# A two-layer memory-attention network on one core: the order in which the steps are recorded, from a list scheduler to a list in the source

## The chip, the cores and the metric

The kernel runs on one core of a Trainium2 chip. The metric is the device time of one execution in microseconds, and the median of the runs where there are several. The profile is of one execution, taken by the hardware profiler; its span runs from the first to the last instruction.

## The reference

The input x has 2048 tokens of 640 features, in bf16. Two rounds of the same pair of blocks are computed, with the same weights:

```
x = x + A(layernorm(x));  x = x + B(layernorm(x));  x = x + A(layernorm(x));  x = x + B(layernorm(x))

A:  q, k, v = x @ wq, x @ wk, x @ wv          32 heads of 20 features, 4 segments of 512 tokens
    for each segment s, in order:
        a_dot = softmax(q k^T * scale + causal mask) @ v           inside the segment
        a_mem = (phi(q) @ M) / (phi(q) @ z + 1e-6)                 what earlier segments left
        o     = g * a_mem + (1 - g) * a_dot                        g = sigmoid(beta), for each head
        M    += phi(k)^T @ v;   z += sum(phi(k))                   phi(t) = t + 1 if t > 0, else exp(t)
    return o @ wo
B:  relu(x @ w1) @ w2                         w1: 640 x 1728, w2: 1728 x 640
```

## The kernel before

The work goes by round (a = 0, 1) and segment (s = 0 to 3), with 512 tokens in each of these eight parts. The heads are taken in groups of four, eight groups to a segment, and two groups share one pad.

The data takes this way in a part. Layernorm statistics are made on DVE (L795, L797), the reciprocal root on GpSimd (POOL, L811), the normalized tokens on DVE (L841) and their transposition by a DMA on SP's queue (`turn`, L817); for the first 512 tokens TensorE (PE) transposes (L866, `first_tile`). The projections of K and Q (`proj_first`, `proj_one`; copied out of PSUM at L981 by DVE or L982 by ACT) and of V (`proj_v`, L1036) are groups of matmuls (`group`, L774 and L777). `spill` (L1070) writes K and Q to a scratch in HBM and `fill` (L1117) reads them back into a pad, in four pieces for each pad, so that each head starts at its own quarter of the partitions; the first pad is filled directly (L1097). `scores` (L1301) multiplies K by Q on four row groups of PE at once, two halves at a time: 160 such pairs of halves in all, five to a pad. `exps` (L1365) takes the exponentials on ACT, `causal` (L1377) masks on POOL, `apply` (L1397, or by token at L1436 for two groups) multiplies by V on column groups, and the result is copied out (L1407), transposed by a DMA and divided (`divide`, L1483 to L1491). The memory is read by `mem_read` (L1180 to L1195), added by `combine` (L1510), and written by `mem_write` (L1238 to L1265) from phi(K) (`phi_`, L1144 to L1147). `turn_o` transposes the result in two DMAs, `out_proj` multiplies it by wo and DVE adds it to x (L1519). `ln_b` normalizes again, `ffn` does block B in groups of matmuls, with the relu on ACT (L1595) or DVE (L1594) and the sum into x on DVE (L1614); `ffn_rest` (L1572, L1579) does the last 64 columns of w1. `store` (L1646) writes out.

PE runs matmuls in three forms. A group of matmuls can be recorded full, 128 x 128, or quartered by columns, each matmul as four of 128 x 32 (`either` gives both; L774 is the full form, L777 the quartered one). `apply` is always quartered, `scores` always in row groups.

Each of these functions is a generator, a stream, that yields its steps one by one. A step names its engine, what it waits for and the buffer it takes. 39 streams are added in a fixed sequence, and a stream can spawn a child with steps of its own (the copy out of PSUM behind a group, for example). `Sched.run` records steps, one at a time, into the program of their engine. The engines then run freely against each other and are held only by semaphores. So the recording decides three things: the order of the steps on each engine (the DMA queue of SP among them), for a copy out of PSUM whether ACT or DVE does it, and for a group's matmul whether it is full or quartered.

The scheduler keeps estimated times for every step. At each turn it computes for the next step of every stream when it could start, adds a lateness where its data would only just be there (`_late`, `SOFT`, `SOFT_DMA`, the latter two from a certain score on), adds an offset from the table `SHIFT` for this stream, part and place, and records the step with the lowest sum:

```
key = (round(start + late + SHIFT.get(self.place(n, st[1]), 0)), 0.5 if op.urgent else prio, self.rank[id(st[1])], n)
if best is None or key < best[0]:
    best = (key, st, end, start, k, op)
```

Of the kernel before, what the change touches and what calls it, by code (L numbers as in the profile page):

```python
# [109 lines left out]
class Op:  # L110

    def __init__(self, alts, waits, dma=None, acq=None, urgent=False, take=(), mode="full", lag=0.0, port=False):
        self.lag = lag
# [8 lines left out]
        self.urgent = urgent  # L125
        self.take = take
        self.data = 0.0
# [32 lines left out]
class Spawn:  # L160
    def __init__(self, prio, gen):
        self.prio = prio
        self.gen = gen


LONE_NS = 300.0
SWITCH_NS = 96.0
COLS_LAG = 1500.0
SOFT = 400
SOFT_DMA = 1000  # L170
SOFT_FROM = ("sc",6,4,1)
SEM_NS = 60.0
PE_MARGIN = 80.0
HOLDERS = 1
SHIFT = {
# [45 lines left out]
class Sched:  # L221


    def __init__(self, prog):
# [9 lines left out]
        self.landed = set()  # L234
        self.met = {}
        self.seen = {}
        self.phase = {}
        self.made = {}
        self.held = {"dve": [], "pool": []}

# [1504 lines left out]
```

## Time and profile before

| | |
|---|---|
| median of 3 runs | 550.78 us (549.76 to 551.34) |
| the profiled execution | span 549.3 us; its time isn't given apart, the span lies 1.5 us under the median |
| PE busy | 539.8 us (98%), 9025 matmuls |
| DVE, ACT, POOL busy | 427.8, 406.0, 195.7 us |
| moved by DMA | 62.20 MB in 133325 packets |

The lines of the profile read like this: line of the kernel, engine, operation, what it writes and what it reads, shape, count, then busy time, mean duration in ns, and the engine's idle time ahead of it with what ended it. PE is matmul, PEld its weight load, SPq the issue of a DMA on SP's queue. A line of the instructions in order of time starts with its start and its length in us. In the waits the numbers are: us in total, times, longest us.

### The profile page before, as it was taken

What the parts mean: (1) busy time and instruction counts of PE and PEld (TensorE: products, weight loads), DVE (VectorE), ACT (ScalarE), POOL (GpSimd) and SP (SyncE); (2) the same over time, 40 slices, a digit from 0 to 9 for tenths busy, and PEclk for the clock granted to TensorE, in tenths of its full rate; (3) what the DMA queues carried; (4) which work ended last, traced back from release to release, by engine and by line L of the source; (5) the groups of instructions that cost most, each with busy time, mean ns of one, the idle gap of its engine ahead of it and who ended that gap; (6) DMA issues with size and microseconds to landing.
All of it is one profiled execution on the core that took longest, in us unless ns stands there. A gap on an engine that the chain in (4) does not pass through costs nothing.

```text
span 549.3 us, 20483 instructions
## 1 busy us (share of the span) xinstructions
PE 539.8 (98%) x9025; PEld 305.5 (56%) x9025; DVE 427.8 (78%) x1067; ACT 406.0 (74%) x516; POOL 195.7 (36%) x305
## 2 busy tenths in 40 slices
PE   7999999999999999999999999999999999999997
PEld 6543464455554546646556555564646654757656
DVE  4899999898999989898778858997899788417102
ACT  5699899789888987788888867897778787350130
POOL 5255444333453334443433423433333333201000
PEclk9999999999999999999999999999999999999999
DMA  8699979715384175438384743336246511541201
GB/s 270 165 198 253 245 158 223 221 44 116 89 165 98 40 180 77 75 68 120 47 212 93 116 116 93 58 69 104 50 139 130 117 32 22 106 63 33 71 2 51
DMA packets 133325, 62.20 MB, mean 113 GB/s; under 512 B 112116, under 2 KB 123124, under 8 KB 133236
## 3 DMA queue, kind: packets, MB, share of 16 engines
q1 hardware_dynamic: 132672, 60.36, 51.5%
q8 instruction: 71, 1.16, 0.9%
q10 hardware_dynamic: 564, 0.53, 0.4%
q14 instruction: 18, 0.15, 0.1%
HBM read 20.56 MB, written 12.85 MB: 61 GB/s over the span
## 4 chain that ended last, share of the span: by engine, by line
PE 88%; ACT 6%; DVE 2%; DMA 2%; SPq 1%; issue 0%
PE ps L774 35%; PE ps L777 35%; PE ps L1301 8%; PE ps L1397 6%; ACT PT L1365 5%; PE ps L1180 2%; DMA x_sb<-in_A_x_dram 1%; PE ps L1572 1%; PE ps L1238 1%; DMA pad<-scr 1%; SPq L602 1%; DVE xn_tok L841 0%; SPq L612 0%; DVE stats L795 0%; DVE x_sb L1614 0%; DVE o_sb L1491 0%
## 5 line engine op out<-in xcount | busy, mean ns | idle before, releaser
L1365 ACT ACTIVATE PT<-ps 128x1024 bf16<-128x1024 f32 x320 | 308.9, 1028 | 59.3 <-PE ps L1301 57.6
L1377 POOL TENSOR_SCALAR_AFFINE_SELECT PT<-PT 128x512 bf16<-128x512 bf16 x256 | 169.3, 679 | 241.1 <-ACT PT L1365 241.0
L777 PE MATMUL ps<-xnT,w_r 128*32 128x512 bf16 x1256 | 76.0, 379 | 0.0
L777 PE MATMUL ps<-w_r,hT 128*32 128x320 bf16 (+1 forms) x1764 | 67.8, 295 | 0.0
L1614 DVE TENSOR_TENSOR x_sb<-x_sb,ps 128x320 bf16<-128x320 bf16 (+1 forms) x65 | 30.7, 474 | 43.6 <-PE ps L777 38.7
L1301 PE MATMUL ps<-pad 20*128 20x512 bf16 (+3 forms) x1024 | 63.4, 301 | 1.2 <-ACT PT L1365 0.7
L774 PE MATMUL ps<-w_r,hT 128*128 128x320 bf16 x404 | 64.2, 300 | 0.0
L795 DVE BATCH_NORM_STATS2 stats<-x_sb 128x6 f32<-128x320 bf16 x124 | 55.0, 478 | 3.8 <-DMA x_sb<-in_A_x_dram 3.0
L777 PEld LDWEIGHTS ps<-w_r,hT 128*32 128x32 bf16 x1764 | 45.2, 97 | 12.6 <-issue 1.4
L1595 ACT ACTIVATE hT<-ps 128x512 bf16<-128x512 f32 x50 | 29.9, 599 | 29.0 <-PE ps L777 25.6
L774 PE MATMUL ps<-xnT,w_r 128*128 128x512 bf16 x206 | 50.8, 380 | 0.0
L774 PEld LDWEIGHTS ps<-w_r,hT 128*128 128x128 bf16 x404 | 37.6, 98 | 19.4 <-issue 4.9
L1301 PEld LDWEIGHTS ps<-pad 20*128 20x128 bf16 x1024 | 17.9, 92 | 52.9 <-issue 24.5
L777 PEld LDWEIGHTS ps<-xnT,w_r 128*32 128x32 bf16 x1256 | 31.6, 97 | 27.8 <-issue 2.0
L1519 DVE TENSOR_TENSOR x_sb<-x_sb,ps 128x320 bf16<-128x320 bf16 x64 | 29.7, 478 | 20.4 <-PE ps L777 16.0
L811 POOL TENSOR_TENSOR rstd<-lnU,mhalf 128x2 f32<-128x2 f32 (+2 forms) x27 | 21.1, 782 | 63.5 <-DVE lnU L807 60.4
L1407 DVE CAST otu<-ps 128x512 bf16<-128x512 f32 x52 | 35.6, 685 | 9.1 <-PE ps L1397 8.2
L1397 PE MATMUL ps<-PT,v_aug 128*21 128x128 bf16 (+3 forms) x896 | 40.3, 300 | 0.0
L1594 DVE TENSOR_SCALAR hT<-ps 128x512 bf16<-128x512 f32 x54 | 36.5, 681 | 1.7 <-PE ps L774 0.7
L1491 DVE TENSOR_TENSOR o_sb<-otk,rden 128x320 bf16<-128x320 bf16 x62 | 34.8, 588 | 0.5
L981 DVE CAST stg<-ps 128x512 bf16<-128x512 f32 (+1 forms) x37 | 24.7, 669 | 12.5 <-PE ps L774 6.3
L1146 ACT ACTIVATE stg<-stg 128x512 bf16<-128x512 bf16 x50 | 31.7, 635 | 2.0 <-DVE rtmp L1144 1.8
(118 smaller groups left out, 731.5 us busy)
## 6 DMA issues: line engine op xcount, KB each, us to landing
pad<-scr SPq DMA_DIRECT2D x124, 80.0 KB
scr<-stg SPq DMA_DIRECT2D x34, 256.0 KB, 2.5
out_dram<-x_sb SPq DMA_DIRECT2D x15, 160.0 KB, 1.9
w_r<-in_B_w_dram SPq DMA_DIRECT2D x10, 216.0 KB, 4.0
w_r<-in_B_w_dram SPq DMA_DIRECT2D x13, 160.0 KB, 2.8
x_sb<-in_A_x_dram SPq DMA_DIRECT2D x10, 160.0 KB, 3.2
scr<-w_r SPq DMA_DIRECT2D x5, 256.0 KB, 4.2
wv_r<-in_A_wv_dram SPq DMA_DIRECT2D x1, 800.0 KB, 9.7
```

What stands on the lines that cost most here:

```text
L774: return e.matmul(view(dst.ap, b), a, b, start=(k == 0), stop=(k == last))
L777: return e.matmul(view(dst.ap[rows], b), part, b, start=(k == 0), stop=(k == last))
L795: tk = yield dve(320, 1, lambda e, c2=c2: e.bn_stats(stats6[:, t, c2, :], x_sb[:, t, c2 * 320:(c2 + 1) * 320]), xt)
L1146: te = yield act(512, lambda e, q=q: e.activation(q, q, ACT.Exp), [tr] + p, psum=False)
L1301: fns.append([(lambda e, z=z, j=j, hh=hh, N=N, o=o, sl=sl, q=hh % 2: e.matmul(slot.ap[:, q, o:o + N], sl.ap[32 * hh:32 * hh + DH, z, 0, 12 ...
L1365: tx = yield act(1024, lambda e, dst=dst, src=src: e.activation(dst, src, ACT.Exp, scale=SCALE), sc + pw)
L1377: tm = yield pool(600.0, lambda e, reg=reg: e.affine_select(out=reg, in_=reg, pattern=[[0, 4], [1, 128]], compare_op=ALU.is_ge, fill=0.0, ...
L1397: fns.append((lambda e, OD, j=j, hh=hh: e.matmul(OD.ap[32 * hh:32 * hh + DH + 1, 128 * j:L], VAUG[vx(a, s)][:, j, 4 * g + hh, :], pt.ap[:, ...
L1407: te = yield evac(L, 1, lambda e: e.tensor_copy(dst, OD.ap), lambda e: e.activation(dst, OD.ap, ACT.Copy), [tk] + OTU[0].tks)
L1491: to = yield dve(320, 1, lambda e, z=z, dst=dst: e.tensor_tensor(dst, av[:, z, :, :, 0:DH], rd.ap[:, z].to_broadcast([128, NJ, 4, DH]), AL ...
L1594: th = yield evac(512, 1, lambda e: e.tensor_scalar(hT[:, dc, :], bk.ap[:, :], 0.0, None, ALU.max), lambda e: e.activation(hT[:, dc, :], b ...
L1614: ta = yield dve(n, 1, lambda e: e.tensor_tensor(x_sb[:, t, c0:c0 + n], x_sb[:, t, c0:c0 + n], bk.ap[:, 0:n], ALU.add), [tk], urgent=True)
```

## The change

The scheduler goes, with its table of offsets, its priorities and its lateness. `ORDER`, a list in the source, names the stream of each of the 5068 steps in the order of recording. A number under 40 is a stream (0 scores, 1 exps, 3 apply, 12 fill, 28 proj_first, 29 and 30 proj_one of K and Q, 31 proj_v, 32 ffn, 33 ffn_rest, 38 the late loads); 40 more is the first unfinished child of that stream; 80 more chooses the other form, DVE in place of ACT or quartered in place of full; `*n` repeats. `_times` still keeps estimated times, by which the buffer that came free first is taken.

```
-                key = (round(start + late + SHIFT.get(self.place(n, st[1]), 0)), 0.5 if op.urgent else prio, self.rank[id(st[1])], n)
-                if best is None or key < best[0]:
-                    best = (key, st, end, start, k, op)
...
+ORDER = """
+35*2 37 35 37 36*2 21 37*2 21 36*3 37 21*2 26*2 21 37 21*2 37 26 21*3 22*3 23 66 23 66 26 22 108 26 28*3 24 26 23 24
+28 68 28 66 28*3 66 104 28 68 28*2 25 28*3 68 28*5 148 28*5 25 148 28*5 68 28*5 68 105 28*4 36 28 68 28*5 68 28 37 28
...
+152 112*6 152 112*10 72 34*7
+"""
...
+    def run(self):
+        tops = list(self.streams)
+        first = tops[0]
+        self._settle_all()
+        for word in ORDER.split():
+            code, _, count = word.partition("*")
+            for _ in range(int(count or 1)):
+                n, other = int(code) % 80, int(code) >= 80
+                st = tops[n] if n < 40 else next(x for x in self.kids[id(tops[n - 40])] if not x[3])
+                self._record(st, st[1].fn() if isinstance(st[1], Either) else st[1], other)
+                self._settle(st)
+                self._settle_all()
+                if isinstance(first[1], Either):
+                    first[1].fn()
+        assert not self.streams
```

Around it some things are said in the streams that the scheduler's order had implied: buffers that are first written by a constant (`VA`, `PTS[0]`) start out taken, `spill` and `mem_write` ask for the event of the part before by name (`Need`) in place of looking whether it has been recorded, and counts of finished children go through `S.meet`. The matmuls that warm PE up at the start write into four other banks of PSUM instead of one; the number of instructions on PE for them is the same:

```
-        def warm_mm(e):
-            return e.matmul(ps[:, 0, 0:128], warm_w, warm_w, start=True, stop=True)
+        def warm_mm(e, k=0):
+            return e.matmul(MISC[k // 4 % 4].ap[:, 128 * (k % 4):128 * (k % 4) + 128] if k < 16 else ps[:, 0, 0:128],
+                            warm_w, warm_w, start=True, stop=True)
```

The steps themselves and what they compute are the same.

More of the change, by code (lines that the diff above doesn't have):

```diff
@@ L110, with __init__ @@
 class Op:
-    def __init__(self, alts, waits, dma=None, acq=None, urgent=False, take=(), mode="full", lag=0.0, port=False):
-        self.lag = lag
+    def __init__(self, alts, waits, dma=None, acq=None, take=(), mode="full", port=False):
         self.port = port
@@ L454, in pe, with _times @@
-def pe(ns, fns, waits=(), acq=None, take=(), mode="full", lag=0.0):
-    return Op([("pe", ns, fns, 190.0)], waits, acq=acq, take=take, mode=mode, lag=lag)
+    def _times(self, op, k, waits):
+        e, hold, fns, tail = op.alts[k]
+        m = PE_MARGIN if e == "pe" else 0.0
+        if e == "pe" and op.mode == "cols" and op.cols_ns is not None:
+            hold = op.cols_ns
+        if e == "pe" and op.mode != self.mode:
+            hold = hold + SWITCH_NS
+        start = max([self.at(t) + SEM_NS + m for t in waits], default=0.0)
+        start = max(self.free[e], start)
+        if e == "dve" and op.port:
+            for a, b in self.held["pool"][-6:]:
+                if a <= start + 66.0 < b:
+                    hold = max(hold, b - start + op.data - 70.0)
+        if e == "pool":
+            for a, b in self.held["dve"][-6:]:
+                if a < start + hold and b > start:
+                    hold = hold + b - max(a, start)
+        return start, start + hold
@@ new lines, in _record @@
+    def _record(self, st, op, other):
+        k = int(other and len(op.alts) > 1)
+        e, _, fns, tail = op.alts[k]
+        if op.cols is not None:
+            op.mode = "cols" if other else "full"
+            fns = op.cols if other else fns
+        waits, slot = op.waits, None
+        for s in op.take:
+            s.free = False
+        if op.acq is not None:
+            slot = self._pick(op.acq)
+            slot.free = False
+            waits = waits + slot.tks
+            fns = [(lambda eng, fn=fn, slot=slot: fn(eng, slot), mark) for fn, mark in fns]
+        start, end = self._times(op, k, waits)
+        self.P.waits(e, waits)
+        self.free[e] = end
+        if e == "pe":
+            self.mode = op.mode
+        if e == "dve" and op.port:
+            self.held[e].append((end - op.data, end))
+        elif e == "pool":
+            self.held[e].append((start, end))
+        if op.dma is not None:
+            tk = self.P.dma(e, fns[0][0], op.dma)
+            self.dma_free = max(self.dma_free, start + 300.0) + tail[1]
+            self.t[(id(tk[0]), tk[1])] = max(self.dma_free, end) + tail[0]
+            if tail[2]:
+                self.free[e] = max(end, self.dma_free)
+            out = tk
+        else:
+            marks = []
+            for fn, mark in fns:
+                tk = self.P.op(e, fn, mark)
+                if tk is not None:
+                    self.t[(id(tk[0]), tk[1])] = end + tail
+                    marks.append(tk)
+            out = marks[0] if len(marks) == 1 else (marks or None)
+        st[1], st[2] = None, ((slot, out) if slot is not None else out,)
@@ L458, in either, with pe @@
+def pe(ns, fns, waits=(), acq=None, take=(), mode="full"):
+    return Op([("pe", ns, fns, 190.0)], waits, acq=acq, take=take, mode=mode)
 def either(op, cols, ns=None):
@@ L1609, in ffn @@
             hrest = yield Need("hR", b, s)
-            sums = [[] for _ in range(NJ)]
             def residual(i, hf, bk, tk, c0, n):
@@ new lines, in items @@
+        def items(f, count):
+            for n in range(count):
+                yield from f(n)
+        S.add(scores())
+        S.add(exps())
+        S.add(items(causal, NSEG * G))
+        S.add(items(apply, 2 * NSEG * G))
+        S.add(each(free_v))
+        S.add(items(turn_pair, NSEG * G))
+        S.add(items(divide, NSEG * G))
+        S.add(each(turn_o))
+        S.add(each(out_proj(0)))
+        S.add(each(out_proj(1)))
+        S.add(each(ln_b(0)))
+        S.add(each(ln_b(1)))
+        S.add(each(fill))
@@ L1712, in bass_interleave_layers__memory_aug_infini_attn__dense_activation_relu__prompt_kernel @@
+        S.add(each(proj_v))
+        S.add(each(ffn))
+        S.add(each(ffn_rest))
+        S.add(each(store))
+        S.add(warm_pe())
+        S.add(consts())
+        S.add(loads())
+        S.add(late_loads())
         S.run()
```

479 lines of the change are left out of this document (194 added, 285 removed), and 41 rows, old and new, of the table SHIFT.

## The prediction

> **What bounds the kernel now.** I read the page's top first, then a table of the span in six stages, then the chain of waits and the instructions in order of time around the places where TensorE (PE) stops.
>
> ```profile
> span 549.3 us, 20483 instructions
> PE 539.8 (98%) x9025; PEld 305.5 (56%) x9025; DVE 427.8 (78%) x1067; ACT 406.0 (74%) x516; POOL 195.7 (36%) x305
> 0.00:20.00 20.00, 16.37 (x162) 12.50 (x162) 12.06 (x36) 9.89 (x27) 8.06 (x26) 1.00 0.73 223
> 20.00:34.00 14.00, 13.97 (x150) 7.00 (x146) 12.81 (x38) 13.23 (x19) 5.81 (x8) 1.00 0.88 187
> 34.00:66.00 32.00, 29.98 (x440) 13.39 (x440) 30.38 (x75) 29.56 (x34) 18.33 (x28) 1.00 1.07 252
> 66.00:430.00 364.00, 363.19 (x5652) 198.48 (x5654) 316.92 (x782) 303.17 (x372) 144.86 (x216) 1.00 0.55 112
> 430.00:475.00 45.00, 45.00 (x783) 25.74 (x779) 35.22 (x89) 33.47 (x39) 17.25 (x28) 1.00 0.27 62
> 475.00:549.30 74.30, 71.28 (x1856) 48.40 (x1848) 20.39 (x52) 16.65 (x29) 1.39 (x2) 1.00 0.23 47
> ```
>
> The table's columns are stage, length, then busy time of PE, weight load, DVE, ACT, POOL, the granted clock (1.00 throughout) and the DMA share. PE is the bound. It idles 9.5 us in all: 3.6 in the first 20 us, 2.0 between 34 and 66, 0.8 in the 364 us after that, 3.0 at the end, where the last sums are stored. An order can only win idle time back, or change how often PE changes its tiling; from 66 us on there is nearly nothing to win and much to lose.
>
> What stands behind the 2.0 us is ACT: from 33.84 it runs thirty exponentials in one piece, and PE waits before scores.
>
> ```profile
> 33.84 27.65 ACT L1365 ACTIVATE PT<-ps 128x1024 bf16<-128x1024 f32 x30
> PEld ps L1301 <- ACT PT L1365: 4.8, 13, 0.5
> 58.91 0.40 PE L1301 MATMUL ps<-pad 20*128 20x384 bf16 x8
> 65.24 0.39 PE L1301 MATMUL ps<-pad 20*128 20x512 bf16 x4 [0.43 <-DMA pad<-scr]
> 65.67 1.02 ACT L1365 ACTIVATE PT<-ps 128x1024 bf16<-128x1024 f32 x1 [1.56 <-PE ps L1301]
> ```
>
> The second row (from the waits of the first 66 us) says that weight loads of scores waited 13 times for exponentials, 4.8 us together; part of it is hidden behind the matmul before, so PE lost less. The last three rows: the 20th pair of score halves starts at 58.91, the 21st only at 65.24, held by its pad.
>
> **How the list is read.** Each number in ORDER is a stream, and a stream's n-th appearance is its n-th step, which is the same step as before. So each engine's order can be read off and set beside the order that the trace shows. The reading can be anchored: a +80 on streams 28 to 32 means quartered matmuls, and proj_v's count before must be 85.
>
> ```profile
> L777 PE MATMUL ps<-wv_r,xnT 128*32 128x320 bf16 x248 | 10.7, 300 | 0.3 <-DVE M_sb L1256 0.3
> L777 PE MATMUL ps<-wv_r,hT 128*32 128x320 bf16 x92 | 4.2, 300 | 0.0
> ```
>
> 248 and 92 quarters are 85 matmuls; the list has 111, which is 31+80, 132 times. So it is another order, and not the old one written down. It is near the old one, though: scores, exponentials and projections come in the same succession, and counted in PE work each score pair stands within 1.5 us of its old place.
>
> **1. Tiling changes.** PE runs in three forms: full, quartered by columns, and by rows (the scores).
>
> ```profile
> 19.08 0.84 PE L774 MATMUL ps<-wv_r,xnT 128*128 128x320 bf16 x5
> 19.85 0.39 PE L1301 MATMUL ps<-pad 20*128 20x512 bf16 x4
> 21.73 0.84 PE L774 MATMUL ps<-wv_r,xnT 128*128 128x320 bf16 x5
> 22.41 0.38 PE L774 MATMUL ps<-xnT,wk_r 128*128 128x512 bf16 x1
> ```
>
> Five matmuls take 22.41 - 21.73 = 0.68 us to the next start where the form stays, and 19.85 - 19.08 = 0.77 where rows follow: a change costs 0.09 us. The old order has 322 of them, the list 330: ten more before the 21st pair, two fewer after it, +0.8 us if none fell into a wait. The Trainium skill, in TensorEngine Tiling (Array Packing), under Key Properties, says that changing the tiling mode drains TensorE. It gives no figure; by that rule each of the ten extra changes is pure loss, and the 0.09 us that the trace shows is its size here. Most of them stand where PE would wait for ACT anyway; they are inside the times of step 3. Quartered or full, a matmul streams alike, so 1378 quartered steps in place of 1279 cost nothing themselves.
>
> **2. The start.** The transposes of token tile 2 move from after the 25th first projection matmul to after the 4th, and the first V copy from DVE to ACT.
>
> ```profile
> 9.00 0.45 PE L774 MATMUL ps<-xnT,wq_r 128*128 128x128 bf16 x5 [0.59 <-DMA wq_r<-in_A_wq_dram]
> 10.12 0.44 PE L866 MATMUL ps<-om_sb,xn_tok 128*128 128x128 bf16 x5
> 10.40 0.33 PE L774 MATMUL ps<-xnT,wq_r 128*128 128x128 bf16 x3
> 17.31 1.04 PE L774 MATMUL ps<-xnT,wq_r 128*128 128x512 bf16 x4 [0.44 <-DVE w_r L1036]
> ```
>
> The transposes take 10.40 - 10.12 = 0.28 us and now fit into the 0.59 us wait for the Q weights. The last row is a wait for the V copy, which stood behind statistics on DVE; on ACT it would start some 0.2 us earlier, and a short wait for tile 2's copy goes too. I take -0.6, from -1.0 to 0: the rest of the 3.6 us is loads and the normalization chain, whose order hardly changes.
>
> **3. The ACT-bound stage.** Ahead of the thirty exponentials the list takes three copies off ACT and adds two short steps.
>
> ```profile
> 18.16 0.20 ACT L715 ACTIVATE gt<-ps 128x32 f32<-128x32 f32 x1 [3.52 <-issue]
> 22.63 0.44 ACT L1036 ACTIVATE w_r<-ps 128x320 bf16<-128x320 f32 x1
> 28.37 0.44 ACT L1036 ACTIVATE v_aug<-ps 128x320 bf16<-128x320 f32 x1
> 30.78 0.60 ACT L982 ACTIVATE stg<-ps 128x512 bf16<-128x512 f32 x1
> 474.76 0.60 ACT L1407 ACTIVATE otu<-ps 128x512 bf16<-128x512 f32 x1 [2.81 <-PE ps L1397]
> ```
>
> Off: 0.44 + 0.44 + 0.60. On: the 0.20 of L715, moved behind the first exponentials, and one copy like the last row's, 0.60. That is -0.7 on the engine that sets the pace here. With the start's 0.6 the 20th pair comes at 58.9 - 1.3 = 57.6. The 21st waits for its pad:
>
> ```profile
> 55.53 1.17 SPq L1117 DMA_DIRECT2D pad<-scr  x3
> 56.74 1.93 SPq L817 DMA_TRANSPOSE otk<-otu  x1
> 58.71 1.06 SPq L643 DMA_DIRECT2D w_r<-in_B_w_dram  x2
> 59.81 0.91 SPq L1070 DMA_DIRECT2D scr<-w_r  x2
> 60.76 0.44 SPq L1117 DMA_DIRECT2D pad<-scr  x1
> 60.76 4.43 DMA pad<-scr
> 59.24 1.18 PE L1436 MATMUL ps<-w_r,PT 128*128 128x21 bf16 x40
> ```
>
> Three pieces went out at 55.53; the fourth stood on SP's queue behind a transpose, two loads of the FFN weights (paced by exponentials) and two spills, and landed 4.43 us after issue. In the list the transpose still stands between the pieces, but loads and spills don't, and ten FFN loads fewer have been issued by then, at a DMA share of 1.07. So the last piece goes out near 59 and lands by 61 to 63. From the 20th pair to the 21st the old order took 65.24 - 58.91 = 6.3 us, of which some 0.6 were waits: 5.7 of work. In the list four K matmuls of 512 columns (0.68 / 5 x 512 / 320 = 0.22 each), one V matmul (0.14) and 12 steps of values by token (the last row is eight of them, 1.18) have moved behind the 21st pair, together 0.9 + 0.1 + 1.3 to 1.8; I take 2.3 off, 3.4 is left, and the pair is due at 57.6 + 3.4 = 61.0. Over the whole list up to there, PE has then done 1.8 us less work than at 65.24 before: the 2.3 less 0.5 that were put ahead of the 20th pair (tiling changes aren't counted as work). If the pad is there, 65.2 - 61.0 - 1.8 = 2.4 us are won, start included; each us by which the pad is late costs one. Both ends: 0 with a pad at 63.4, and 2.7 if no wait is left.
>
> **4. After 66 us.** Two tiling changes fewer: -0.2. Against it, leads are spent. SP's queue now has 20 of 31 pads whose four pieces are split by other steps, 7 before. Most pads still lead their scores by 3 us and more, but one doesn't:
>
> ```profile
> 408.97 3.76 SPq L1117 DMA_DIRECT2D pad<-scr  x10
> 426.21 2.91 SPq L817 DMA_TRANSPOSE oT<-o_sb  x2
> 429.46 0.40 PE ps L1301 x4
> ACT PT L1365 <- PE ps L1301: 57.6, 109, 1.6
> PE ps L1301 <- DMA pad<-scr: 0.4, 1, 0.4
> ```
>
> The pad of the 146th pair (429.46) was filled within the 408.97 row; in the list three pieces follow the first oT transpose of the 426.21 row. They can't go out before about 427.6, half of that row on, and need a landing of the kind of the 4.43 us: 2.5 us late if DVE reaches its part of that transpose no sooner. But the list puts fewer other DVE steps ahead of it, so I take 0.2, from 0 to 2.5. ACT gets 5.8 us more to do ahead of the 145th pair, taken from DVE's share or moved forward; its waits for scores (57.6 us in 109, 0.5 each) hide about one copy of 0.6 between two pairs; where there are two, PE waits: 0.2 (0 to 1).
>
> **Sum.** -2.4 - 0.2 + 0.4 = -2.2 us: a span of 547.1. The span lies 1.5 us under the median of 550.78, which I keep: 548.6 us, -0.4%. A difference under 0.3%, 1.65 us, is about what a measurement of this kernel can't tell from none. The queues' own order costs nothing on SP, whose issues lie under PE's work wherever the pad leads.
>
> **Rivals.**
> *The stage wins nothing.* For it: the 21st pair's pad is a DMA matter (share 1.07, 4.43 us), and the FFN loads not issued there come later, beside the next pads. Then only the start and the two changes count, less the new waits: 550.8 - 0.6 - 0.2 + 0.4, about 550.4. Against it: what stood ahead of the last piece for 2 us has left.
>
> *Late pads: slower.* Thirteen more pads are split, behind transposes that wait for DVE results. Where the last piece lands after PE has reached its pair, ACT starves as at 65.67 and PE idles 0.43 us or more, as at 65.24. If all thirteen did, 13 x 0.43 = 5.6: 548.6 + 5.6 = 554.2. It turns the sign from six upward (2.6 us), and past 0.3% from nine. Against it: of the seven old split pads one alone made PE wait (the 0.4, once), and the list leaves most others 3 us or more.
>
> **How the numbers follow.** The forecast has 0.66; its spread reaches over the 0.3% line, which takes 0.11. The stage that wins nothing has 0.16, late pads 0.18. So faster 0.55, within 0.3% 0.27, slower 0.18. Low end: the 2.0 us of 34 to 66, the 0.8 after it and over half of the first 3.6 all gone, 550.8 - 4.8 = 546.0. High end: somewhat over half of the late pads' price beyond the forecast, reached from nine or ten of them, 552.8. That leaves about 0.1 on each side.
>
> **What would show it.** Right: PE idle in the stage to 66 us falls from 2.0 to under 1, the 21st pair starts near 61, L1301's waits for DMA vanish there, and the 66 to 430 stage keeps idle under 1.5 us. Wrong: the 21st pair still starts past 63 with a DMA wait; or L1301 shows DMA waits at several later pairs, the 146th first; or PE busy time grows by more than the 0.8 us of tiling changes.

## The result and the profile after

The kernel after takes 553.14 us (median of 11 runs, 552.05 to 554.65), the kernel before 550.89 us on the same chip (549.76 to 552.01): a ratio of 1.004, 95% interval 1.0028 to 1.0053. It is slower, by 0.4%; the prediction said faster by 0.4%.

First the top of the page and the table of the six stages, after. The columns are those of the prediction's table: stage, length, busy time of PE, weight load, DVE, ACT, POOL, the granted clock, the DMA share.

```profile
span 552.1 us, 21028 instructions
PE 541.5 (98%) x9298; PEld 306.5 (56%) x9298; DVE 420.7 (76%) x1073; ACT 400.3 (73%) x510; POOL 194.7 (35%) x305
```

```profile
0.00:20.00 20.00, 18.06 (x177) 13.91 (x178) 13.40 (x41) 11.64 (x28) 8.59 (x26) 1.00 0.80 245
20.00:34.00 14.00, 13.87 (x302) 7.05 (x300) 13.60 (x36) 12.96 (x18) 6.06 (x11) 1.00 0.78 173
34.00:66.00 32.00, 31.16 (x461) 14.15 (x463) 29.98 (x76) 31.02 (x37) 17.92 (x27) 1.00 0.87 191
66.00:430.00 364.00, 358.74 (x5729) 194.70 (x5722) 295.40 (x755) 300.42 (x375) 140.86 (x210) 1.00 0.53 113
430.00:475.00 45.00, 44.99 (x689) 25.04 (x685) 32.82 (x85) 33.26 (x39) 18.60 (x29) 1.00 0.29 57
475.00:552.10 77.10, 74.68 (x1964) 51.66 (x1956) 35.54 (x85) 11.02 (x18) 2.62 (x4) 1.00 0.30 68
```

Length less PE gives the idle time. Up to 66 us it is 1.94 + 0.13 + 0.84 = 2.9 us, 5.7 before: the part that the change was forecast to win, it won. From 66 to 430 us it is 5.26, 0.81 before: there 4.5 us went. Less is left at the end (2.4 for 3.0), and PE is busy 1.7 us more. One caution goes with these numbers: this execution took 554.26 us, 1.1 above the median of its kernel (in the runs here the time is the span and some 2.1 us, which puts the profiled execution of the kernel before, with its span of 549.3 us, at some 551.4). The profile of one version below, list_before, fell in a slower state of the chip (681 us at a granted clock of 0.755) and is left out wherever profiles are compared.

The instructions in order of time show the stage that the forecast was about: the 20th and the 21st score pair on PE, the last three pieces of the 21st pair's pad on SP, the exponentials on ACT.

```profile
57.00 0.40 PE L1278 MATMUL ps<-pad 20*128 20x384 bf16 x8
...
60.37 0.39 PE L1278 MATMUL ps<-pad 20*128 20x512 bf16 x4
...
55.46 1.27 SPq L1091 DMA_DIRECT2D pad<-scr  x3
...
46.50 12.94 ACT L1340 ACTIVATE PT<-ps 128x1024 bf16<-128x1024 f32 x14 [0.17 <-PE ps L1278]
```

The 21st pair starts 4.9 us earlier than before and waits for nothing; the thirty exponentials end at 59.4, 2 us earlier.

The waits of PE from 66 to 430 us, after; the same question to the kernel before has two rows, 0.5 and 0.3 us. The numbers are total, times, longest.

```profile
PE ps L751 <- DVE M_sb L1233: 1.5, 1, 1.5
PE ps L1547 <- DVE stg L956: 1.0, 1, 1.0
PE ps L1278 <- ACT PT L1340: 0.8, 1, 0.8
PE ps L1372 <- DVE mv L774: 0.5, 1, 0.5
PE ps L751 <- DVE stg L956: 0.4, 1, 0.4
PE ps L751 <- DMA oT<-o_sb: 0.4, 1, 0.4
PE ps L754 <- DVE x_sb L1494: 0.2, 1, 0.2
```

Seven single waits, none of them for a pad. (Lines are those of the new source: L751 and L754 are the full and the quartered matmuls, L1278 the scores, L1547 `ffn_rest`.) The instructions around the two longest, PE first, then DVE, then SP:

```profile
157.86 0.31 PE L751 MATMUL ps<-wv_r,xnT 128*128 128x320 bf16 x1 [1.49 <-DVE M_sb L1233]
...
153.85 0.48 DVE L1010 CAST v_aug<-ps 128x320 bf16<-128x320 f32 x1
156.63 0.42 DVE L1121 TENSOR_TENSOR phs<-stg,rtmp 128x512 bf16<-128x512 bf16 x1 [2.30 <-DMA phk<-phs]
...
157.18 0.63 DVE L1233 TENSOR_TENSOR M_sb<-M_sb,ps 128x462 f32<-128x462 f32 x1
...
146.91 4.61 SPq L794 DMA_TRANSPOSE xnT<-xn_tok  x2
151.56 1.32 SPq L794 DMA_TRANSPOSE phk<-phs  x1
...
88.25 0.73 PE L1547 MATMUL ps<-xnT,w_r 128*32 128x256 bf16 x20 [1.02 <-DVE stg L956]
...
79.17 1.95 SPq L619 DMA_DIRECT2D w_r<-in_B_w_dram  x3
81.16 4.96 SPq L794 DMA_TRANSPOSE xnT<-xn_tok  x2
```

PE waits at 156.4 for a PSUM bank that the addition into the memory on DVE (L1233) frees. DVE had stood still since 154.3, because the phi step ahead of that addition in its queue needed a buffer that a phk transpose was still reading, and that transpose stood on SP behind two xnT transposes. At 87.2 the FFN's first step begins to wait, and the trace names a copy on DVE that had ended 2 us before its start. What came last was the second of the two xnT transposes issued from 81.16 on, behind the FFN loads: it landed at 88.00, 0.25 us ahead of the step. That the name is an accident is also seen when the same wait comes up in other kernels below: there the trace names M_sb, rtmp, or "issue" for it.

### The profile page after: what moved, and what is told of

It is laid out like the page before. It is cut to its first block, busy times and chain, and to the rows that moved or that the text cites. A ratio compares the mean times of both kernels' runs of the same rounds, so it can differ in the third digit from the quotient of the medians.

```text
span 552.1 us, 21028 instructions
## 1 busy us (share of the span) xinstructions
PE 541.5 (98%) x9298; PEld 306.5 (56%) x9298; DVE 420.7 (76%) x1073; ACT 400.3 (73%) x510; POOL 194.7 (35%) x305
## 4 chain that ended last, share of the span: by engine, by line
PE 82%; DVE 12%; DMA 4%; ACT 1%; issue 0%; POOL 0%; SPq 0%; DVEq 0%
PE ps L751 33%; PE ps L754 33%; PE ps L1278 8%; PE ps L1372 5%; DMA phk<-phs 2%; DVE stats L772 2%; PE ps L1154 2%; DVE phs L1121 1%; DVE xn_tok L818 1%; DVE o_sb L1466 1%; DMA oT<-o_sb 1%; DVE rtmp L1118 1%; DMA otk<-otu 1%; DVE hT L1569 1%; DVE stg L956 1%; DVE x_sb L1588 1%
## 5 line engine op out<-in xcount | busy, mean ns | idle before, releaser
L754 PE MATMUL ps<-xnT,w_r 128*32 128x512 bf16 x1312 | 82.1, 380 | 0.1
L754 PE MATMUL ps<-w_r,hT 128*32 128x320 bf16 (+1 forms) x1820 | 75.6, 296 | 0.0
L751 PE MATMUL ps<-w_r,hT 128*128 128x320 bf16 x390 | 66.7, 300 | 0.0
L1278 PE MATMUL ps<-pad 20*128 20x512 bf16 (+3 forms) x1024 | 63.4, 301 | 1.0 <-ACT PT L1340 1.0
L1570 ACT ACTIVATE hT<-ps 128x512 bf16<-128x512 f32 x43 | 25.6, 603 | 50.2 <-PE ps L754 48.9
L1569 DVE TENSOR_SCALAR hT<-ps 128x512 bf16<-128x512 f32 x61 | 41.7, 684 | 26.5 <-PE ps L754 18.6
L772 DVE BATCH_NORM_STATS2 stats<-x_sb 128x6 f32<-128x320 bf16 x124 | 56.3, 476 | 3.1 <-DMA x_sb<-in_A_x_dram 2.9
L754 PEld LDWEIGHTS ps<-w_r,hT 128*32 128x32 bf16 x1820 | 45.9, 97 | 14.2 <-issue 2.8
L751 PE MATMUL ps<-xnT,w_r 128*128 128x512 bf16 x192 | 51.6, 380 | 0.0
L754 PEld LDWEIGHTS ps<-xnT,w_r 128*32 128x32 bf16 x1312 | 32.8, 96 | 30.8 <-issue 4.6
L751 PEld LDWEIGHTS ps<-w_r,hT 128*128 128x128 bf16 x390 | 36.1, 98 | 19.0 <-issue 4.9
L1278 PEld LDWEIGHTS ps<-pad 20*128 20x128 bf16 x1024 | 17.8, 92 | 48.2 <-ACT PT L1340 23.5
L956 DVE CAST stg<-ps 128x512 bf16<-128x512 f32 (+2 forms) x46 | 29.9, 652 | 11.1 <-PE ps L754 7.6
L751 PE MATMUL ps<-wo_r,oT 128*128 128x320 bf16 x192 | 37.5, 300 | 0.5 <-DMA oT<-o_sb 0.4
```

The costliest lines, as they stand in the source:

```text
L751: return e.matmul(view(dst.ap, b), a, b, start=(k == 0), stop=(k == last))
L754: return e.matmul(view(dst.ap[rows], b), part, b, start=(k == 0), stop=(k == last))
L772: tk = yield dve(320, 1, lambda e, c2=c2: e.bn_stats(stats6[:, t, c2, :], x_sb[:, t, c2 * 320:(c2 + 1) * 320]), xt)
L956: te = yield evac(N, 1, lambda e: e.tensor_copy(sg.ap[:, t0:t0 + N], bk.ap[:, 0:N]), lambda e: e.activation(sg.ap[:, t0:t0 + N], bk.ap[:, ...
L1278: fns.append([(lambda e, z=z, j=j, hh=hh, N=N, o=o, sl=sl, q=hh % 2: e.matmul(slot.ap[:, q, o:o + N], sl.ap[32 * hh:32 * hh + DH, z, 0, 12 ...
L1569: th = yield evac(512, 1, lambda e: e.tensor_scalar(hT[:, dc, :], bk.ap[:, :], 0.0, None, ALU.max), lambda e: e.activation(hT[:, dc, :], b ...
```

## The experiments

Theories at the outset. **A**: the early gain is real, and single late places behind it lose it; put them right and it stays. **B**: PE's own work (tiling changes, quartered matmuls). **C**: PE's advance is only borrowed, and is lost where PE next meets a chain that hasn't advanced. **D**: the list as such costs something. Ratios are to the kernel before, run together with each version on the same chip. In the diffs a line is a stretch of ORDER with one word for each step.

### The old order as a list

```
-ORDER: as given
+ORDER: the 5068 steps in the order that the list scheduler of the kernel before recorded
```

> The code of the kernel after, but its list holds the order that the list scheduler of the kernel before recorded, step for step (322 tiling changes, 9025 matmuls). If the loss of the kernel after lies in its order (theory A), this is the kernel before again: ratio 1.000, 550.9 us, at most 0.7 us off. If the list itself or the code around it costs something (theory D), it stays near the kernel after: 553 us, ratio 1.004.

Measured: 551.26 us, ratio 1.0007 (0.9992 to 1.0023). D falls: the loss is in the order.

### The new front, and the new rest

```
front_new:  new order up to the 21st score pair, then what is left, in the old order
rest_new:   old order up to the 21st score pair, then what is left, in the new order
```

> The new order up to the 21st score pair (60 us), and behind it all steps that are left in the order of the kernel before (332 tiling changes, 9154 matmuls). Theory A (the front of the new order gains, and single late places behind 66 us lose it): PE's idle time up to 66 us stays at 2.9 us as in the kernel after, that from 66 to 430 us at 0.8 us as before, so about 2.8 us less idle, less 10 tiling changes at 0.09 us: 549.0 us (548.2 to 550.0), ratio 0.9965. Theory B (PE's own work: tiling changes and quartered matmuls): about 0.9 us slower than before, 551.8 us. Theory C (the front borrows from what comes behind, whatever the order there): no faster than before, 550.5 to 552, with a stall of 1 us or more near 88 us, where the FFN starts.

> The order of the kernel before up to the 21st score pair (65 us), and behind it all steps that are left in the new order (320 tiling changes, 9169 matmuls). Theory A: PE's idle time behind 66 us is that of the kernel after, 4 to 5 us; with the old front 554.5 us (553 to 556), ratio 1.0065; the stall at the start of the FFN (1.0 us) can be smaller, since the old front has issued the FFN loads already. Theory B: two tiling changes fewer than before and fewer quartered matmuls than after: 550.5 us. Theory C (the loss in the rest is what the front borrowed): about 551 us.

Measured: front_new 556.34 us, 1.0105 (1.0088 to 1.0122); rest_new 554.57 us, 1.0073 (1.0056 to 1.0089). The rest came out as A said: behind the old front, which has no advance to borrow, it still loses, and C (about 551 us) falls for it. Set beside the kernel after (1.0040), the same rest with the old front is 0.0033 slower, 1.8 us: that is what the new front is worth there, as far as the two intervals let one say. The front with the old rest was far off for every theory. Its instructions on PE and SP in order of time, and a table by stage:

```profile
72.12 1.17 PE L1205 MATMUL ps<-w_r,phk 128*128 128x147 bf16 x8 [4.44 <-DMA phk<-phs]
...
57.70 4.85 SPq L612 DMA_DIRECT2D w_r<-in_B_w_dram  x10
62.60 1.02 SPq L1037 DMA_DIRECT2D scr<-w_r  x2
63.66 2.60 SPq L787 DMA_TRANSPOSE xnT<-xn_tok  x1
66.31 3.67 SPq L787 DMA_TRANSPOSE phk<-phs  x1
```

```profile
67.70:72.10 4.40, 0.00 (x0) 0.00 (x0) 0.87 (x3) 1.96 (x3) 1.22 (x2) 0.79 1.19 183
72.10:77.00 4.90, 4.88 (x28) 2.60 (x29) 1.87 (x5) 0.85 (x2) 0.00 (x0) 0.50 1.03 201
```

The new front leaves ten FFN loads unissued; the old rest then issues them in one piece, and the transposes of xnT and phk behind them come late: one wait of 4.44 us. And after it PE's clock was at 0.50 for 4.9 us, so the wait cost about half as much again (estimated as half of these 4.9 us). The new front was also cut off just ahead of the 21st pair, which the old rest brings only at 63.80.

### Five places moved

```
-0 30 11 15 38 15 16 38       30 12 2 150       30 16 1 ... 150 110 3 10 16 110
+0 30 11    38    16 38 10    30 12 2 150 15 15 30 16 1 ... 150 110 3    16 110
-71 111 11    11 0 150 ... 111 1 111 19 16 83
+71 111 11 19 11 0 150 ... 111 1 111    16 83
-112 2 15 15 6 112 112 ... 112 112 15 112 6 12 ... 112 12 1       112 72 83
+112 2 15    6 112 112 ... 112 112    112 6 12 ... 112 12 1 15 15 112 72 83
-12 30 32 11 32 32 0 ... 2 2 72    27 2 2
+12 30 32    32 32 0 ... 2 2 72 11 27 2 2
```

> The new order with five single places moved, each ahead of a wait of PE: the xnT transpose of the first half ahead of two pads and three FFN loads on SP (1.0 us at 88 us); the phk transpose ahead of one xnT transpose on SP (1.5 us at 158 us); a phi step behind two exps on ACT (0.8 us at 249 us); one K/Q copy ahead of two phi steps on DVE (0.4 us at 84 us); one residual addition ahead of one normalization on DVE (0.5 us at 299 us). Tiling changes (330) and matmuls (9298) are unchanged. Theory A: each wait goes, 4.2 us in all: 549 us (548 to 550.5), ratio 0.9965 to the kernel before, PE idle from 66 to 430 us about 1.1 us. Theory B (tiling changes, quartered matmuls): 553 us still. Theory C2 (the waits only move to the next late step): 551.5 us or more, with idle of over 3 us in that stretch.

Measured: 554.33 us, 1.0069 (1.0051 to 1.0087), no better than the kernel after. The waits of PE from 66 to 430 us:

```profile
PE ps L751 <- DMA oT<-o_sb: 1.5, 1, 1.5
PE ps L754 <- DVE x_sb L1588: 1.2, 1, 1.2
PE ps L1212 <- DMA phk<-phs: 0.5, 1, 0.5
...
```

The waits at 84, 88, 158 and 249 us are gone, 3.7 us, and in their place stand three others of 3.2 us, all for transposes (the second again names DVE; it is an xnT transpose landing). C2 had this right. Two of the moves had put back a step that feeds a transpose; six_moves below leaves those two out.

### SP steps alone, and six places

```
sp_moves:   the first two line pairs above, without the words 15
six_moves:  sp_moves, the words 15 of the first pair, and
-112 72 112    27 6 83 ... 112 112 2 15 15 6
+112 72 112 15 27 6 83 ... 112 112 2    15 6
-32 32 0    20 112 112 ... 2 2 2 72 27 2 2
+32 32 0 72 20 112 112 ... 2 2 2    27 2 2
-3 112 100 27 0 6 32 ... 1 32 11 27 32 1 6 32 6       32 27 10
+3 112 100    0 6 32 ... 1 32 11    32 1 6 32 6 27 27 32 27 10
```

> The new order with two SP steps moved and nothing else: the xnT transpose of the first half ahead of two pads and three FFN loads, and the phk transpose ahead of one xnT transpose. Theory A (single late places, with slack behind them): the stalls of 1.0 us near 88 us and 1.5 us near 158 us go and nothing comes in their place, 550.6 us (549.8 to 551.6), ratio 0.9995. Theory C2 (a wait taken away comes back at the next late step): 552.5 us or more, with new waits of 2 us in all behind 158 us. Theory B (PE's own work): 553 us.

> The new order with six single places moved, chosen so that no step that feeds an SP transpose is put back: the two SP moves; the Q copy ahead of two phi steps (0.4 us); at 249 us a phi step on DVE moved forward by one normalization, so that ACT reaches the exps earlier, in place of the phi step put behind the exps; at 299 us the residual addition ahead of the scaling of the memory, not of the normalization; at 302 us two statistics steps behind the divisions that feed the oT transpose. Theory A': the waits that came up in the run with five moves (1.5 us for the oT transpose at 256 us, 1.2 us for the xnT transpose at 305 us) were of those moves' own making, so here 4 of the 4.6 us go: 549.1 us (548 to 550.5), ratio 0.997, PE idle from 66 to 430 us under 1.5 us. Theory C2: the chains over DVE and SP behind these places are themselves late, whatever is moved: 551.5 us or more, idle there 3 us or more.

Measured: sp_moves 553.29 us, 1.0047 (1.0029 to 1.0065); six_moves 552.67 us, 1.0044 (1.0027 to 1.0060). Neither is distinguishable from the kernel after. With six places mended PE waits thus from 66 to 430 us:

```profile
PE ps L1547 <- DVE rtmp L1118: 1.7, 1, 1.7
PE ps L754 <- DVE mv L774: 0.8, 1, 0.8
...
```

The FFN's first step waits 1.7 us although its first transpose goes out 3 us earlier, at 77.84:

```profile
80.41 1.30 SPq L619 DMA_DIRECT2D w_r<-in_B_w_dram  x3
82.34 1.88 SPq L794 DMA_TRANSPOSE xnT<-xn_tok  x1
...
88.56 0.71 PE L1547 MATMUL ps<-xnT,w_r 128*32 128x256 bf16 x17 [1.69 <-DVE rtmp L1118]
```

The second transpose, issued at 82.34 right behind three loads, took until 88.3 to land. A in its simple form (put single late places right and the gain stays) falls with these two runs.

### Fewer tiling changes, and a hundred more

```
few_changes:      14 words of streams 28 to 31 between 7 and 53 us: 80 more or 80 less (320 changes of 330)
hundred_changes:  in the old order, 50 words 32 (one full FFN step among others) become 112 (quartered)
```

> The new order with nothing moved; 14 steps of PE take the other tiling, which leaves 320 tiling changes of 330 (9316 matmuls for 9298). If a change costs 0.09 us wherever it lies (step 1 of the prediction), PE's busy time falls by 0.9 us and the time to 552.2 us (551.5 to 552.9), ratio 1.0025; if changes hide beside waits or weight loads, 553.1 us.

> The order of the kernel before with 50 single FFN steps between 98 and 470 us taken in the quartered tiling among full ones, so 422 tiling changes for 322 and 150 matmuls more (9175). Theory of the prediction's step 1 (each change costs 0.09 us wherever it lies): PE's busy time grows by 9 us, 560 us (559.0 to 561.0), ratio 1.017. If changes hide beside weight loads: 552 us or less. If each also loses a lead elsewhere: over 562 us.

Measured: few_changes 554.32 us, 1.0075 (1.0048 to 1.0102), against 552.2 or 553.1 expected, so it misses both: ten changes fewer in the first 53 us gave no gain that can be seen. It decides little, since its runs lie from 553.65 to 558.25, and the profiled one, the slowest, reached the first score pair 2.0 us later than the kernel after, had PE's clock at 0.50 from 8.1 to 11.6 us and lost 2.1 us in three waits for pads. hundred_changes is clear: 560.96 us, 1.0166 (1.0142 to 1.0189), 9.6 us between the medians for 100 changes, 0.096 each, 0.09 by the ratio. These changes lie among FFN steps between 98 and 470 us, and 50 of the matmuls are quartered besides. That the quartering is free is seen in new_fifty (below): there 50 changes with only nine more quartered matmuls cost 4.8 us against the kernel after (1.0127 less 1.0040), 0.096 each again. At that price the eight more of the new order are 0.8 us of its 2.25; for the ten that lie ahead of the 21st pair the price isn't shown, as few_changes decides little.

### The loads moved off the transposes

```
front_loads, against front_new:  -2 38 38 38*8 13 13 27 ... 2 8 12      8 8 31
                                 +2 38 38      13 13 27 ... 2 8 12 38*8 8 8 31
front_both, besides:             -9 12 8    12 1 8 ... 10 0 3 19 8 10
                                 +9 12 8 19 12 1 8 ... 10 0 3    8 10
```

> The run with the new order up to the 21st score pair and the old order behind it, with eight FFN loads on SP moved behind the phk and oT transposes and four pads, where the new order has loads too. That run had one wait of 4.4 us for the phk transpose behind those loads, and after it PE's clock was at 0.5 for 5 us. Theory A (the front gains 1.5 to 2.8 us if the loads are kept off the transposes): both go, 556.3 less 4.4 less 2.7: 549.0 us (548 to 550.3), ratio 0.9965. Theory C (the front only borrows): the loads then stop a transpose or the FFN's start later, PE idle from 66 to 430 us over 2 us, 550.9 us or more.

> The new order up to the 21st score pair, the old order behind it, with both phk transposes that waited behind FFN loads (4.4 us in the first such run, 3.9 us in the second) now ahead of eight of the loads and of ten pads. Theory A: without the wait and without the stretch at half clock behind it, 556.0 less 3.9 less 2.6: 549.5 us or less, ratio 0.998. Theory C: the loads now stand ahead of the xnT transpose of the FFN's first step, as in the kernel after, a wait of 1 to 2 us near 88 us: 550.6 us (549.8 to 552), ratio 1.000. If the wait at any one place is over 3.4 us, the clock falls again and the time is over 554 us.

Measured: front_loads 556.04 us, 1.0095 (1.0075 to 1.0115); front_both 553.90 us, 1.0050 (1.0028 to 1.0071). PE in front_loads, then in front_both:

```profile
84.89 0.95 PE L1205 MATMUL ps<-v_aug,phk 128*32 128x147 bf16 x46 [3.85 <-DMA phk<-phs]
```

```profile
90.34 0.73 PE L1540 MATMUL ps<-xnT,w_r 128*32 128x256 bf16 x20 [2.38 <-issue]
```

The wait went from the second phk transpose (4.44 us at 72) to the third (3.85 at 85) to the xnT transpose of the FFN's first step (2.38 at 90), each time the next transpose behind the loads. So the eight loads cost something at each of these three places: in the old order they stand among the pads of the ACT-bound stage, in the new one ahead of the FFN's transposes. That what the new front gains is in part this, as C says, is likely; how large a part isn't shown. Both came out slower than C's numbers, in part since these waits halved the clock as well, the one of 2.38 us too (the last section). That isn't all: the four of twelve executions of front_both whose clock stayed at 1.00 took 552.0 to 554.1 us, for 549.8 to 552 expected.

### The old order mended

```
old_front_mended:  -28 28 27     27 28 12 28 27 28 151 31 31    -27 38 0    6 30 83 12    -27 0 27    38 3 3 ... 1 27 31 12
                   +28 28 27 151 27 28 12 28 27 28     31 31    +27 38 0 83 6 30    12    +27 0 27 12 38 3 3 ... 1 27 31
old_all_mended:    besides, two exps ahead of a phi step, one M addition ahead of a statistics step, 320 tiling changes
```

> The order of the kernel before with three moves in its first 65 us, one for each of three waits of PE in its trace (0.44 us at 17.3, 0.52 us at 56.4, 0.43 us at 65.2): the first V copy ahead of two statistics steps on DVE, a copy of an attention output ahead of a division on DVE, one pad ahead of two FFN loads on SP. Theory A (what PE gains early it keeps): 1.1 us faster, 549.4 us (548.8 to 550.2), ratio 0.998. Theory C (an advance of PE alone is lost where PE next waits for a chain of normalization on DVE, transpose on SP and landing, which the advance does not move): the first FFN step at 89.4 us started 0.09 us behind the landing of its xnT transpose, so a wait of 0.5 to 1.0 us comes up there: 550.2 us, ratio 0.9995.

> The run with three early moves in the old order, and besides: two exps ahead of a phi step on ACT at 427 us (a wait of 0.5 us), the addition of the memory ahead of a statistics step on DVE at 150 us (0.3 us), and 320 tiling changes for 322 (0.2 us). Theory A: 2.1 us faster than before, 548.4 us (547.6 to 549.6), ratio 0.996. Theory C: the early moves give nothing, the later ones 0.3 to 0.8 us: 549.9 us (549.2 to 550.6), ratio 0.9985.

Measured: old_front_mended 551.58 us, 1.0002 (0.9984 to 1.0019); old_all_mended 550.81 us, 0.9991 (0.9972 to 1.0009). Three waits of 1.4 us in all were taken on, and no gain came of it; in the trace of the first a new wait stands just behind the stage:

```profile
69.74 0.69 PE L1204 MATMUL ps<-w_r,phk 128*128 128x147 bf16 x8 [0.76 <-DMA phk<-phs]
```

That is C's way, though not at C's place. No version beat the kernel before by more than can be measured.

### The new order with PE slowed

If C holds strictly, a slower PE should wait less.

```
-ORDER: as given
+25 words of stream 32 (one FFN step among others of its form) between 100 and 295 us in the other tiling
```

> The new order with nothing moved; 25 single FFN steps between 100 and 295 us take the other tiling, which makes 380 tiling changes of 330 (9325 matmuls for 9298), 50 x 0.096 = 4.8 us more PE work: 1.5 us of it ahead of the wait at 158 us, 2.3 between that and the wait at 249 us, 1.0 ahead of those at 299 and 307. Theory C (PE waits there for chains over DVE, ACT and SP's transposes that do not follow PE's pace, so a slower PE waits less): the four waits of 3.2 us in all go, idle from 66 to 430 us falls from 5.3 to under 2.5 us, and the 4.8 us cost only 1.6: 554.8 us (554 to 556), ratio 1.007. Theory A (each late step hangs on PE steps and moves with them): the waits stay, idle stays at 5 us: 557.9 us (557 to 559), ratio 1.0127.

Measured: 558.08 us, 1.0127 (1.0108 to 1.0146): A's number to the digit. Yet its trace has C's idle time from 66 to 430 us (two rows of the table by stage, then a row of PE in order of time):

```profile
66.00:430.00 364.00, 361.97 (x5755) 193.03 (x5746) 295.28 (x752) 298.98 (x373) 139.85 (x210) 1.00 0.54 112
430.00:475.00 45.00, 43.98 (x665) 24.25 (x662) 31.84 (x85) 32.92 (x39) 16.90 (x27) 1.00 0.35 63
```

```profile
435.27 0.39 PE L1278 MATMUL ps<-pad 20*128 20x512 bf16 x4 [0.74 <-DMA pad<-scr]
```

Only 2.0 us there, but 1.0 in the next stage (none in the kernel after), 0.74 of it for the pad of the 146th pair (last row); and the FFN's first step (at 87.87) doesn't wait at all, although up to 100 us this kernel is the kernel after, step for step. So one trace doesn't tell which waits belong to the order. Four profiles do, all with the new order of steps behind 66 us and nothing moved there (few_changes and new_fifty differ from the kernel after only in the tiling of some steps, rest_new in its front; waits in us, places by the times of the kernel after):

| the wait of PE, at about | after | few_changes | new_fifty | rest_new |
|---|---|---|---|---|
| 84 us, a Q copy on DVE | 0.4 | 0.4 | 0.4 | 0.4 |
| 88 us, the FFN's first step | 1.0 | none | none | none |
| 158 us, the addition into the memory | 1.5 | none | none | none |
| 249 us, exponentials on ACT | 0.8 | 0.8 | none | 0.8 |
| 299 us, a sum into x on DVE (the trace names mv) | 0.5 | 0.2 | 0.2 | 0.5 |
| 307 us, the oT transpose | 0.4 | 0.9 | 0.8 | 0.5 |
| 314 us, a sum into x on DVE | 0.2 | 0.2 | 0.2 | 0.2 |

The two longest waits of the profile after, the ones that sp_moves was made for, are in none of the other three: that sp_moves won nothing is no wonder. The five small ones come back nearly every time, 1.6 to 2.5 us together, where PE in the kernel before idles 0.8 us in all from 66 to 430 us.

### What stands when executions are put together

The stage tables give PE's idle time for four executions in the old order (before, old_front_mended, old_all_mended, hundred_changes) and six in the new (after, five_moves, sp_moves, six_moves, few_changes, new_fifty). Means in us, with the range:

| stage | old order | new order | difference |
|---|---|---|---|
| to 66 us | 5.3 (4.3 to 6.7) | 3.7 (2.4 to 5.4) | -1.6 |
| 66 to 430 | 0.8 (0.3 to 1.7) | 3.7 (2.0 to 5.3) | +2.8 |
| 430 to 475 | 0.2 (0 to 0.5) | 0.4 (0 to 1.2) | +0.2 |
| behind | 2.7 (2.5 to 3.0) | 2.9 (2.4 to 3.7) | +0.2 |
| eight tiling changes | | | +0.8 |

The sum is 2.4 us; the medians differ by 2.25. From 66 to 430 us the two ranges don't meet, so the loss there is a property of the order, whatever single places are mended. And it belongs to the rest of the order and not to the front ahead of it. The waits of PE from 95 to 430 us, behind the seam, in front_new (new front, old rest), then in rest_new (old front, new rest):

```profile
PE ps L747 <- DVE M_sb L1226: 0.3, 1, 0.3
```

```profile
PE ps L1277 <- ACT PT L1339: 0.8, 1, 0.8
PE ps L1371 <- DVE mv L773: 0.5, 1, 0.5
PE ps L750 <- DMA oT<-o_sb: 0.5, 1, 0.5
PE ps L753 <- DVE x_sb L1493: 0.2, 1, 0.2
```

PE's idle time in this stretch is 0.2 to 0.8 us in the seven profiles with the old rest (the three with the new front have 0.3 each) and 1.5 to 3.8 us in the seven with the new rest (2.05 with the old front). So theory C, that the rest only pays back what the front borrowed, doesn't hold behind 95 us.

The sum of 2.4 comes close to the 2.25 in part by luck: in single executions PE's whole idle time differs by 2.8 us among the four and by 5.1 among the six.

What makes the rest wait more can be counted from the records of before and after: for each PE step between 66 and 475 us, its start less the end of the last DVE step that it waits for. Of 306 such steps before and 300 after (by the waits that the two programs hold) 4 and 31 have less than 0.2 us, 25 and 97 less than 0.5 us. For ACT (the scores left out) it is 2 and 21 under 0.5 us, for the DMA landings that the records time (few pads are among them) 4 and 7. The new order takes results as they come; any that is late in an execution stops PE. That the thin leads cause the whole 2.8 us is argued from these counts and not shown: no run widened them all. How the whole loss divides between DVE, ACT and transposes stays open, too; the waits that come back (the table above) are of all three kinds.

## Why the prediction was wrong, point by point

**What bounds it.** Right: PE is the bound before and after, and "from 66 us on there is nearly nothing to win and much to lose" is what happened.

**1. Tiling changes.** The price is right, and now measured by itself: 0.096 us a change among FFN steps, 0.8 us for the eight at that price. The drain that the Trainium skill states in TensorEngine Tiling (Array Packing), Key Properties, has that size in this kernel, also beside other work. PE's busy time grew by 1.7 in the two profiles. The 0.9 beyond is of the size by which it differs between two executions of nearly the same order (539.8 before, 541.3 in old_front_mended, both of 9025 matmuls); where it comes from isn't shown.

**2. The start** and **3. the stage.** Right in mechanism and place. The 20th pair came at 57.00 for 57.6, the 21st at 60.37 for 61.0, its last pad piece went out at 56.4 for 59, and no DMA wait of the scores is left there. Idle time to 66 us fell by 2.8 us in these two executions, 1.6 on average. What I didn't see: the baseline was one execution. In the same order the first score pair starts at 17.74 or at 19.89 us (after and five_moves, alike up to 75 us), as the loads land; a term of 0.6 us for the start can't be read from one profile. The stage itself is steadier: from the first score pair to the 21st it is 45.4 us before and 42.6 after, 44.9 to 45.7 in the four profiles of the old order and 42.6 to 44.1 in the six of the new one.

**4. After 66 us: this step failed.** The sum had +0.4 there for leads spent; it was +2.8 on average, 4.5 in the profiled execution. Two things in it were wrong. I looked for spent leads at pads, and only where the list splits them on SP. The pads held in the profile after; they cost 2.1 us in few_changes and 0.7 in new_fifty, the 146th among them, as forecast. But the other waits were for transposes (xnT, phk, oT) behind loads or each other on the same queue, and for copies and sums on DVE and exponentials on ACT that end with little or no lead ahead of their use. ACT was priced (0.2 us), and one wait of 0.8 us for it came; DVE's own leads and the transposes' had no term at all. And I priced the ten loads as a gain ("ten FFN loads fewer have been issued by then") without following them to where they went: ahead of the FFN's own transposes, where PE waited 1.0 us in the profile after, though not in those of few_changes and new_fifty.

**Sum and range.** With 2.8 in place of 0.4 for step 4, and 1.6 for what steps 2 and 3 give together, the forecast's own sum is -1.6 + 0.8 + 2.8 + 0.4 = +2.4, where 2.25 was measured (the last 0.4 are the two stages behind 430 us). The range ended at 552.8, 0.3 us short. Its upper end took 4.2 of the late pads' 5.6 us, which is three quarters and not "somewhat over half", and still had no room for waits that aren't for pads.

**Rivals.** "The stage wins nothing" is refuted by the 21st pair. "Late pads" had the right side and nearly the right time (554.2), but by luck: no pad was late in the profile after, and in few_changes and new_fifty late pads are 2.1 and 0.7 us of the idle time.

**What would show it.** Of the four signs of a right forecast three came true (idle under 1 us in the stage, the 21st pair near 61, no DMA wait of the scores there); the fourth, idle under 1.5 us from 66 to 430, did not, and that one decided. Of the signs of a wrong one, PE's busy time grew by more than 0.8 us.

## What to carry to other kernels

Where the bound engine is 98% busy, an order can hardly win, and its leads are what it can lose: compare, for the old and the new order, how long each result lies ready before the bound engine takes it, on every engine and queue, before counting any gain. Follow a transfer that has left one stage to the queue position it takes in the next, because transposes behind it pay there. And before a wait in one trace is mended, see whether it is in a second execution: here the two longest were not, while five shorter ones came back nearly every time. Even so, moving single steps at six places moved the median by no more than the measurement could tell, since other waits came up.

## What the runs showed of the hardware

In these records PE's granted clock changes in steps of 3.41 us: it is 0.50 from 91.43 to 94.84 in front_both, from 8.86 to 12.27 in rest_new, from 70.23 to 77.06 in front_new. Three pairs of such stretches show when it falls: front_both around its wait of 2.38 us, the start of rest_new, and the kernel after around its wait of 1.49 us (after the length comes PE's busy time; the clock is third from the end):

```profile
88.02:91.43 3.41, 1.09 (x29) 0.70 (x30) 2.20 (x7) 0.69 (x2) 0.56 (x1) 1.00 1.16 310
91.43:94.84 3.41, 3.41 (x9) 1.23 (x9) 1.51 (x3) 2.46 (x4) 1.23 (x2) 0.50 0.94 266
```

```profile
5.45:8.86 3.41, 1.81 (x24) 1.19 (x21) 1.99 (x6) 2.23 (x7) 1.57 (x4) 1.00 1.00 313
8.86:12.27 3.41, 3.26 (x31) 3.26 (x32) 1.06 (x3) 1.24 (x6) 2.42 (x6) 0.50 1.08 350
```

```profile
155.22:158.63 3.41, 1.81 (x14) 0.75 (x10) 2.00 (x8) 1.34 (x2) 0.00 (x0) 1.00 0.79 177
158.63:162.05 3.42, 3.38 (x56) 1.72 (x60) 2.75 (x9) 3.42 (x5) 2.87 (x4) 1.00 0.02 5
```

In front_both the half clock begins 1.1 us after PE has gone on. In rest_new no single wait of its stretch is over 0.6 us; they add up to 1.6 us of 3.41, and that was enough, as in few_changes (1.6 us idle from 4.73 to 8.14, no wait over 0.74 us, the clock at 0.50 to 11.56). The kernel after had as much idle time, nearly in one piece, and kept its clock, and so did six_moves, whose 1.69 us fell into two stretches. So here it was the idle time within a stretch that mattered and not the length of one wait, with the limit near 1.6 us of 3.41, where both outcomes were seen; 1.46 us (the kernel before, from 4.78 us) left the clock at 1.00. The waits of 3.85 and 4.44 us brought 6.1 and 4.9 us of work at 0.50. The Trainium skill, TensorE: Matmul & The Clock Gate, under Why this matters for your kernels, puts the limit at gaps of about 3 us; the wait of 2.38 us is below that, and here the measurement decides. The 3.4 us that front_both's forecast took as the limit was too high, too.

An issue on SP isn't of fixed length: that of a phk transpose took 1.32 us in the kernel after (the row at 151.56) and 3.67 us in front_new, behind ten loads, two spills and another transpose (66.31), and what stands behind it on SP goes out that much later.
